# Attention and a two-layer GEMM in one kernel: earlier w_in, later w_out, another order of the second GEMM's filling

## The chip, the cores and the metric

One NeuronCore of a Trainium2 chip runs the whole kernel. The metric is the device time of one execution in microseconds; a lower one is better.

## The reference

```python
# q, k, v: (8, 8, 576, 64) fp32; f: (8, 8, 576)
scores = matmul(q, k.T) / sqrt(64)
cum = cumsum(log(clip(f, 1e-4, 1)), axis=-1)
decay = cum[:, :, :, None] - cum[:, :, None, :]
attn = softmax(where(causal, -1e9, scores + decay))
x = matmul(attn, v)            # -> (4608, 512): heads side by side
h = x @ w_in                   # w_in (512, 2048)
out = gelu(h) @ w_out          # w_out (2048, 512), exact gelu; out fp32
```

## The kernel before

The decay splits into a factor for the row, which the normalisation takes out again, and one for the column, which is multiplied into v. So GpSimd or VectorE *weighs* v (`weigh_v`, L228: two heads at a time, bf16, with the weights themselves as a 65th column), and the attention is exp of the scaled scores, a triangular mask, a matmul with the weighed v and a division by the 65th column.

The kernel works on eight batches of 576 tokens for the attention and on nine chunks of 512 tokens for the GEMMs. One batch has four pairs of heads `i`. For a pair there are four score tiles `t` (`scores`, L246): matmuls of kT and qA/qB into a PSUM tile with tag "s" (two buffers), ScalarE's exponential to a tile `e{t}`, GpSimd's mask of the diagonal blocks (L263, one or two instructions). `attend` (L275) multiplies these with the weighed v into a tile with tag "o" (two buffers), `normalize` (L290) divides on VectorE, and `to_xT` (L303) transposes x on TensorE and copies it to `xT_sb`.

`gemm1(c, ffb)` (L314) is one of 16 blocks of the first GEMM: four matmuls of 512 columns into a PSUM tile with tag "m" (two buffers), then gelu on ScalarE into `g_of[c][ffb]`. `gemm2(c)` (L332) is a generator over the 64 matmuls of the second GEMM, four tiles of 128 tokens one after the other with 16 matmuls each; a copy on VectorE and a store on SyncE's queue follow each tile. `take(gen, n)` issues the next n of them.

The order within each engine is the order of the program text. Batch 0 has its own text, `first_attention` (L359). Then, for b = 1 to 7, `attention(b, gemm2(b-1), counts)` (L422) runs with the second GEMM of the chunk before as filling: after score tile t of pair i stand `counts[i][t]` of its matmuls (lists FILL for b = 2 to 7 and FILL_1 for b = 1, L419; row 4 of a list is the end of the attention; what is left over comes at the very end). After each attention comes `gemm1(b, ...)`; among its blocks stand the transposes of q and k of the next batch (`transposes_pe`, L193: TensorE into a buffer with tag "s", eight copies on VectorE) and the weighings of the next batch (blocks 2, 6, 10, 14, on GpSimd). In the first GEMM of chunk 0 the transposes of pairs 0, 1 and 2 of batch 1 stand at blocks 8, 11 and 15; those of pair 3 stand within the attention of batch 1 and use the tag "o".

Which of two buffers a PSUM tile gets is fixed when the program is built, and the waits for it with it.

There are two DMA queues. SyncE's (hardware) loads f and v and stores the result. v has one buffer in `v_pool`, so v of batch b+1 starts when the last weighing of batch b has read its own. GpSimd's (software) loads q, k, w_in and w_out and casts them to bf16; an issue takes GpSimd's time and stands in its order. In `first_attention`, w_in (`load_w_in`, four issues) stands behind `weigh_v(0, 1)`, so behind the first half of v of batch 0. `load_next` issues q and k of batch 1 in two halves of the heads and then w_out (`load_w_out`, four issues of four row blocks); v of batch 1 follows on SyncE's queue in five issues (`load_v(1)`, L455).

Of the kernel before, what the change touches and what calls it, by code (L numbers as in the profile page):

```python
# [8 lines left out]
FP32 = mybir.dt.float32  # L9
# [5 lines left out]
P = 128  # L15
# [34 lines left out]
def kernel(  # L50
# [10 lines left out]
    nc = tc.nc  # L61
# [3 lines left out]
    d_model, d_ff = moe_w_in.shape  # L65
    N_tok = B * S
    n_dm = d_model // P
    n_ff = d_ff // P
    n_sub = TC // P
# [19 lines left out]
    def load_qk_tokens(b, h0=0, h1=H):  # L89

        if b not in qk_of:
            qk_of[b] = [
                qk_pool.tile([PT, H, JT * D], BF16, tag=n, name=f"{n}{b}")
                for n in "qk"
            ]
        for src, dst in zip((q, k), qk_of[b]):
            nc.gpsimd.dma_start(  # L97
                dst[:, h0:h1, :],
                src[b, h0:h1].rearrange("h (p j) d -> p h (j d)", j=JT),
            )  # L100

    def load_v(b, h0=0, h1=H):
        if b >= B:
            return
        if b not in v_of:
            v_of[b] = v_pool.tile([P, H, NBLK, D], FP32, tag="v", name=f"v{b}")
        for n in range(NBLK):
            nc.sync.dma_start(  # L108
                v_of[b][:, h0:h1, n, :],
                v[b, h0:h1, K0[n] : K0[n] + P].rearrange("h p d -> p h d"),  # L110
            )
# [26 lines left out]
    w_out_sb = consts.tile([P, n_ff, d_model], BF16)  # L138
# [3 lines left out]
    def load_w_in(c):  # L142
        f4 = slice(c * d_ff // 4, (c + 1) * d_ff // 4)
        nc.gpsimd.dma_start(w_in_sb[:, :, f4], w_in_r[:, :, f4])

    def load_w_out():
        for kt in range(0, n_ff, 4):
            nc.gpsimd.dma_start(w_out_sb[:, kt : kt + 4, :], w_out_r[:, kt : kt + 4, :])
# [79 lines left out]
    def weigh_v(b, i, eng=None):  # L228

        if b not in vw_of:  # L230
            vw_of[b] = v_pool.tile([P, H, NBLK, D + 1], BF16, tag="vw", name=f"vw{b}")
        hs = slice(2 * i, 2 * i + 2)
        bh = b * H + 2 * i
        w = wT[:, :, bh : bh + 2].rearrange("p n h -> p h n")
        eng = eng or nc.gpsimd
        eng.tensor_tensor(  # L236
            vw_of[b][:, hs, :, 0:D],
            v_of[b][:, hs, :, :],
            w.unsqueeze(3).to_broadcast([P, 2, NBLK, D]),
            Alu.mult,  # L240
        )
        eng.tensor_copy(vw_of[b][:, hs, :, D], w)
# [3 lines left out]
    def scores(b, i, t):  # L246
        st = s_psum.tile([P, 2, 512], FP32, tag="s", name=f"s{t}")
        c = 0
        for n, q0, w in STILES[t]:
            for h, qt in enumerate((qA[i], qB[i])):  # L250
                nc.tensor.matmul(  # L251
                    st[:, h, c : c + w],
                    kT[i][:, K0[n] : K0[n] + P],
                    qt[:, q0 : q0 + w],
                    start=True,
                    stop=True,
                )
            c += w
        et = e_pool.tile([P, 2, 512], BF16, tag=f"e{t}", name=f"e{t}")
        e_of[b, i, t] = et  # L260
        nc.scalar.activation(et[:, :, 0:c], st[:, :, 0:c], Act.Exp, scale=scale)  # L261
        for c0 in SDIAG[t]:
            nc.gpsimd.affine_select(  # L263
                out=et[:, :, c0 : c0 + P],
                in_=et[:, :, c0 : c0 + P],
                compare_op=Alu.is_ge,
                fill=0.0,
                base=0,
                pattern=[[0, 2], [1, P]],
                channel_multiplier=-1,  # L270
            )
# [57 lines left out]
            ]  # L329
        nc.scalar.activation(g_of[c][ffb], ps, Act.Gelu)  # L330

    def gemm2(c):  # L332

        t0 = c * TC
        for ts in range(n_sub):
            ps = m_psum.tile([P, d_model], FP32, tag="m", name="ps2")
            for kt in range(n_ff):
                nc.tensor.matmul(  # L338
                    ps,
                    g_of[c][kt][:, ts * P : (ts + 1) * P],  # L340
                    w_out_sb[:, kt, :],
                    start=(kt == 0),
                    stop=(kt == n_ff - 1),
                )
                if kt == n_ff - 1:
                    ot = o_pool.tile([P, d_model], FP32, tag="ot", name="ot")
                    nc.vector.tensor_copy(ot, ps)  # L347
                    nc.sync.dma_start(
                        out[t0 + ts * P : t0 + (ts + 1) * P, :], ot
                    )  # L350
                yield

    def take(gen, n):
        for _ in range(n):
# [2 lines left out]


    def first_attention():  # L359
        def load_next():  # L360
            load_qk_tokens(1, 0, 4)
            load_qk_tokens(1, 4, 8)
            load_w_out()

        def transposes(i, pool, tag):
            transposes_first(i, 1, pool, tag)
            transposes_first(i, 0, pool, tag)

        def attend_pair(i):
            for h in range(2):  # L370
                attend(0, i, h, (0, 1, 2, 3, 4))
                normalize(0, i, h)

        transposes(0, o_psum, "o")
        scores(0, 0, 0)
        scores(0, 0, 1)
        transposes(1, m_psum, "m")
        psw = o_psum.tile([P, NBLK, BH], FP32, tag="o", name="psw")
        for n in range(NBLK):
            nc.tensor.transpose(  # L380
                psw[:, n, :], wk[:, K0[n] : K0[n] + P], ident_fp[:BH, :BH]
            )
        nc.vector.tensor_copy(wT[:, 0:4, :], psw[:, 0:4, :])
        nc.vector.tensor_copy(wT[D:P, 4, :], psw[D:P, 4, :])
        scores(0, 0, 2)
        scores(0, 0, 3)
        scores(0, 1, 0)
        scores(0, 1, 1)
        transposes(2, m_psum, "m")
        weigh_v(0, 0, nc.vector)  # L390
        weigh_v(0, 1)
        for c in range(4):
            load_w_in(c)
        scores(0, 1, 2)
        scores(0, 1, 3)
        scores(0, 2, 0)
        scores(0, 2, 1)
        transposes(3, m_psum, "m")
        attend_pair(0)
        weigh_v(0, 2, nc.vector)  # L400
        scores(0, 2, 2)
        scores(0, 2, 3)
        weigh_v(0, 3)
        to_xT(0, 0, m_psum, "m")
        scores(0, 3, 0)
        scores(0, 3, 1)
        attend_pair(1)
        scores(0, 3, 2)
        scores(0, 3, 3)
        load_next()  # L410
        attend_pair(2)
        to_xT(0, 1, m_psum, "m")
        attend_pair(3)
        to_xT(0, 2, m_psum, "m")
        to_xT(0, 3, m_psum, "m")

    FILL = [[0, 12, 4, 4], [2, 3, 3, 2], [2, 3, 3, 2], [2, 2, 2, 2], [8, 4, 4, 0]]  # L419
    FILL_1 = [[0, 4, 0, 0], [0, 4, 0, 4], [2, 2, 2, 2], [3, 3, 3, 3], [8, 4, 4, 0]]  # L420

    def attention(b, fill, counts):  # L422
        for i in range(HP):
            for t in range(4):
                scores(b, i, t)
                if i >= 2 and t == 0:
                    to_xT(b, i - 2)
                if i and t == 1:
                    attend(b, i - 1, 0, (0, 1, 2))
                elif i and t == 2:  # L430
                    attend(b, i - 1, 0, (3, 4))
                    normalize(b, i - 1, 0)
                elif i and t == 3:
                    attend(b, i - 1, 1, (0, 1, 2, 3, 4))
                    normalize(b, i - 1, 1)
                if b == 1 and i == 0 and t == 2:
                    transposes_pe(1, 3, in_s=False)
                    load_qk_tokens(2)
                take(fill, counts[i][t])
        i = HP - 1  # L440
        take(fill, counts[HP][0])
        attend(b, i, 0, (0, 1, 2, 3, 4))
        normalize(b, i, 0)
        to_xT(b, i - 1)
        take(fill, counts[HP][1])
        attend(b, i, 1, (0, 1, 2, 3, 4))
        normalize(b, i, 1)
        take(fill, counts[HP][2])
        to_xT(b, i)
        take(fill, 999)  # L450

    for b in range(B):
        if b == 0:
            first_attention()
            load_v(1)  # L455
        else:
            load_v(b + 1)
            attention(b, gemm2(b - 1), FILL_1 if b == 1 else FILL)
        for ffb in range(n_ff):
            gemm1(b, ffb)  # L460
            if b + 1 < B:
                at = (8, 11, 15) if b == 0 else (0, 4, 8, 11)
                if ffb in at:
                    transposes_pe(b + 1, at.index(ffb))
                if ffb % 4 == 2:
                    weigh_v(b + 1, ffb // 4)
        if 0 < b < B - 2:
            load_qk_tokens(b + 2)
    take(gemm2(B - 1), 999)
# [34 lines left out]
```

## Time and profile before

| | us |
|---|---|
| median of 3 runs | 399.92 (399.39 to 400.99) |
| the profiled execution | 400.63 |
| its span, first to last instruction | 398.8 |
| TensorE busy | 369.6 (93%) |
| ScalarE busy | 217.8 (55%) |
| VectorE busy | 203.3 (51%) |
| GpSimd busy | 130.2 (33%) |

The first row stands for the kernel, the second and third for the one execution that the trace shows. Busy times are of an engine over the whole span. The ends of matmuls are modelled and overlap the next one's start, so TensorE's busy time is not its time at full rate.

### The profile page before, as it was taken

To read this page: it belongs to the slowest core of one execution; us is meant where nothing else is said; L and a number is where in the kernel's file an instruction comes from. 1 tells how busy PE (TensorE), PEld (TensorE's weight loads), DVE (VectorE), ACT (ScalarE), POOL (GpSimd) and SP (SyncE) were. 2 spreads that over 40 slices of the span, in tenths; PEclk is the share of its full clock that TensorE was granted. 3 is DMA by queue.
4 is the path that set the end of the run, shared out by engine and by line. 5 is a ranking of instruction groups with operands and counts; after the bars stand their busy time and mean duration, and the time that the engine had idled before them with its cause. 6 is when DMAs were issued, how large, how long until landed. Compare 5 with 4: busy or idle time off the path is not lost.

```text
span 398.8 us, 7577 instructions
## 1 busy us (share of the span) xinstructions
PE 369.6 (93%) x3093; PEld 207.7 (52%) x3093; DVE 203.3 (51%) x448; ACT 217.8 (55%) x293; POOL 130.2 (33%) x261
## 2 busy tenths in 40 slices
PE   2889967999899999999999989999999999999995
PEld 1564434655466546654565546554665466444442
DVE  6473862449535863488247924693459535002011
ACT  4665561706764576646672677357745674630710
POOL 6586037350343323251335133612352142000000
PEclk9999966999999999999999999999999999999999
DMA  7899958727810781148402870178010010001002
GB/s 109 158 173 211 196 96 141 139 81 131 118 54 28 147 123 42 48 100 128 78 28 74 135 125 28 54 131 138 36 54 2 1 54 28 26 27 65 16 28 79
DMA packets 63874, 34.18 MB, mean 86 GB/s; under 512 B 42784, under 2 KB 59168, under 8 KB 63840
## 3 DMA queue, kind: packets, MB, share of 16 engines
q0 software_dynamic: 16896, 13.63, 22.9%
q1 hardware_dynamic: 46944, 20.08, 20.6%
q8 instruction: 24, 0.39, 0.4%
q14 instruction: 10, 0.08, 0.1%
HBM read 37.90 MB, written 9.44 MB: 119 GB/s over the span
## 4 chain that ended last, share of the span: by engine, by line
PE 79%; DVE 8%; DMA 6%; POOL 2%; issue 2%; SPq 1%; ACT 1%; POOLq 0%
PE ps L338 31%; PE ps L318 23%; PE s L251 11%; PE o L282 7%; DMA v<-in_v_dram 5%; PE s_t L209 3%; DVE kT L221 3%; PE ps_x L306 2%; SPq L108 1%; POOL vw L236 1%; DVE qA L221 1%; DVE ot L347 1%; PE ps_f L174 1%; ACT e L261 1%; DVE qB L221 1%
## 5 line engine op out<-in xcount | busy, mean ns | idle before, releaser
L338 PE MATMUL ps<-w_out_sb,g 128*128 128x512 bf16 x576 | 145.4, 383 | 0.0
L330 ACT ACTIVATE g<-ps 128x512 bf16<-128x512 f32 x144 | 86.0, 598 | 106.1 <-PE ps L318 106.1
L261 ACT ACTIVATE e<-s 128x1024 bf16<-128x1024 f32 (+2 forms) x128 | 107.3, 863 | 52.5 <-PE s L251 47.9
L318 PE MATMUL ps<-xT_sb,w_in_sb 128*128 128x512 bf16 x576 | 131.1, 379 | 0.6
L263 POOL TENSOR_SCALAR_AFFINE_SELECT e<-e 128x256 bf16<-128x256 bf16 x160 | 63.7, 413 | 115.0 <-ACT e L261 113.8
L318 PEld LDWEIGHTS <-w_in_sb 128*128 128x128 bf16 x576 | 54.5, 98 | 60.7 <-issue 0.6
L338 PEld LDWEIGHTS <-g 128*128 128x128 bf16 x576 | 50.7, 98 | 42.9 <-issue 1.8
L251 PE MATMUL s<-qA,kT 128*128 128x384 bf16 (+2 forms) x192 | 56.0, 299 | 12.3 <-DVE kT L221 6.9
L347 DVE COPY ot<-ps 128x512 f32<-128x512 f32 x36 | 24.8, 690 | 82.1 <-PE ps L338 81.1
L251 PEld LDWEIGHTS <-kT 128*128 128x128 bf16 x384 | 37.8, 103 | 47.6 <-DVE kT L221 8.0
L221 DVE COPY kT<-s_t 64x288 bf16<-64x288 bf16 x108 | 51.8, 479 | 1.5
L236 POOL TENSOR_TENSOR vw<-v,wT 128x640 bf16<-128x640 f32 x30 | 38.3, 1277 | 42.5 <-PE o L282 22.6
L251 PE MATMUL s<-qB,kT 128*128 128x384 bf16 (+2 forms) x192 | 51.6, 300 | 0.3 <-DVE qB L182 0.3
L282 PE MATMUL o<-vw,e 128*128 128x65 bf16 x960 | 45.2, 196 | 4.5 <-POOL e L263 4.3
L282 PEld LDWEIGHTS <-e 128*128 128x128 bf16 x960 | 41.6, 99 | 12.7 <-POOL e L263 5.4
L295 DVE RECIPROCAL r<-o 128x5 f32<-128x5 f32 x64 | 12.5, 195 | 69.4 <-PE o L282 69.3
L221 DVE COPY qA<-s_t 64x288 bf16<-64x288 bf16 x54 | 25.8, 479 | 14.5 <-PE s_t L209 13.5
L296 DVE TENSOR_TENSOR x<-o,r 128x320 bf16<-128x320 f32 x64 | 31.5, 492 | 2.2
L221 DVE COPY qB<-s_t 64x288 bf16<-64x288 bf16 x54 | 26.0, 481 | 0.7
L97 POOL DMA_DIRECT2D q<-in_q_dram x12 | 9.1, 757 | 45.7 <-PE s_t L209 44.7
L309 DVE COPY xT_sb<-ps_x 128x576 bf16<-128x576 bf16 x32 | 14.5, 452 | 8.3 <-PE ps_x L306 8.3
L306 PE MATMUL ps_x<-ident_bf,x 128*128 128x128 bf16 x160 | 14.4, 220 | 1.8 <-DVE x L296 1.8
(49 smaller groups left out, 133.8 us busy)
## 6 DMA issues: line engine op xcount, KB each, us to landing
out_dram<-ot SPq DMA_DIRECT2D x36, 256.0 KB, 2.0
v<-in_v_dram SPq DMA_DIRECT2D x35, 256.0 KB, 4.8
q<-in_q_dram POOLq DMA_DIRECT2D x6, 576.0 KB, 6.4
k<-in_k_dram POOLq DMA_DIRECT2D x6, 576.0 KB, 8.4
w_in_sb<-in_moe_w_in_dram POOLq DMA_DIRECT2D x4, 512.0 KB, 8.0
w_out_sb<-in_moe_w_out_dram POOLq DMA_DIRECT2D x4, 512.0 KB, 17.3
v<-in_v_dram SPq DMA_DIRECT2D x10, 128.0 KB, 5.4
q<-in_q_dram POOLq DMA_DIRECT2D x4, 144.0 KB, 4.0
```

Of the source, the lines that this page charges most:

```text
L221: nc.vector.tensor_copy(rows[:, odd], ps[odd * D : (odd + 1) * D, h].rearrange("d j p -> d p j"),)
L236: eng.tensor_tensor(vw_of[b][:, hs, :, 0:D], v_of[b][:, hs, :, :], w.unsqueeze(3).to_broadcast([P, 2, NBLK, D]), Alu.mult,)
L251: nc.tensor.matmul(st[:, h, c : c + w], kT[i][:, K0[n] : K0[n] + P], qt[:, q0 : q0 + w], start=True, stop=True,)
L261: nc.scalar.activation(et[:, :, 0:c], st[:, :, 0:c], Act.Exp, scale=scale)
L263: nc.gpsimd.affine_select(out=et[:, :, c0 : c0 + P], in_=et[:, :, c0 : c0 + P], compare_op=Alu.is_ge, fill=0.0, base=0, pattern=[[0, 2], [ ...
L282: nc.tensor.matmul(o[:, m, :], e_of[b, i, t][:, h, c : c + P], vw_of[b][:, 2 * i + h, n, :], start=(n == 0), stop=(n == m),)
L296: nc.vector.tensor_tensor(x_of[b, i][:, :, h, :], o[:, :, 0:D], r.unsqueeze(2).to_broadcast([P, NBLK, D]), Alu.mult,)
L306: nc.tensor.transpose(ps[:, K0[m] : K0[m] + P], x_of[b, i][:, m, :, :], ident_bf)
L318: nc.tensor.matmul(ps, w_in_sb[:, kt, ffb * P : (ffb + 1) * P], xT_sb[:, kt, t0 : t0 + TC], start=(kt == 0), stop=(kt == n_dm - 1),)
L330: nc.scalar.activation(g_of[c][ffb], ps, Act.Gelu)
L338: nc.tensor.matmul(ps, g_of[c][kt][:, ts * P : (ts + 1) * P], w_out_sb[:, kt, :], start=(kt == 0), stop=(kt == n_ff - 1),)
L347: nc.vector.tensor_copy(ot, ps)
```

## The change

- `load_w_in` moves up in `first_attention`: from behind `weigh_v(0, 1)` to behind `scores(0, 0, 2)`, so it no longer stands behind a weighing that waits for v.
- `load_w_out` moves from behind q and k of batch 1 to block 2 of the first GEMM of chunk 0, behind `weigh_v(1, 0)` in GpSimd's order.
- v of batch 1 is loaded in two halves of the heads, five issues each.
- The transposes of q and k of batch 1 stand at blocks 10, 13 and 15 instead of 8, 11 and 15.
- `gemm2` of chunk 0 runs in quarters of w_out: two tiles of tokens are open at once, and each quarter of four row blocks is used for both before the next quarter. The other chunks keep their order.
- FILL's first row is 5, 7, 4, 4 instead of 0, 12, 4, 4. FILL_1 has nothing in its first pair and 2, 2, 2, 2 in the three others.

```diff
-    def gemm2(c):
+    def gemm2(c, quarters=False):
+        if quarters:
+            order = [
+                (t2 + ts, 4 * kq + kt)
+                for t2 in (0, 2)
+                for kq in range(4)
+                for ts in range(2)
+                for kt in range(4)
+            ]
+        else:
+            order = [(ts, kt) for ts in range(n_sub) for kt in range(n_ff)]
...
-            load_w_out()
...
         scores(0, 0, 2)
+        for c in range(4):
+            load_w_in(c)
         scores(0, 0, 3)
...
         weigh_v(0, 1)
-        for c in range(4):
-            load_w_in(c)
...
-        load_next()
+        load_qk_tokens(1, 0, 4)
+        load_qk_tokens(1, 4, 8)
...
-    FILL = [[0, 12, 4, 4], [2, 3, 3, 2], [2, 3, 3, 2], [2, 2, 2, 2], [8, 4, 4, 0]]
-    FILL_1 = [[0, 4, 0, 0], [0, 4, 0, 4], [2, 2, 2, 2], [3, 3, 3, 3], [8, 4, 4, 0]]
+    FILL = [[5, 7, 4, 4], [2, 3, 3, 2], [2, 3, 3, 2], [2, 2, 2, 2], [8, 4, 4, 0]]
+    FILL_1 = [[0, 0, 0, 0], [2, 2, 2, 2], [2, 2, 2, 2], [2, 2, 2, 2], [8, 4, 4, 0]]
...
-            load_v(1)
+            load_v(1, 0, 4)
+            load_v(1, 4, 8)
...
-            attention(b, gemm2(b - 1), FILL_1 if b == 1 else FILL)
+            attention(b, gemm2(b - 1, b == 1), FILL_1 if b == 1 else FILL)
...
-                at = (8, 11, 15) if b == 0 else (0, 4, 8, 11)
+                at = (10, 13, 15) if b == 0 else (0, 4, 8, 11)
...
                     weigh_v(b + 1, ffb // 4)
+                if b == 0 and ffb == 2:
+                    load_w_out()
```

## Rows read from the trace of the kernel before

**Rows 1.** The page's 40 slices of the span: TensorE's granted clock, in tenths.

```profile
PEclk9999966999999999999999999999999999999999
```

**Rows 2.** TensorE's waits, 33 to 103 us: total us, times, longest us.

```profile
PE o L282 <- POOL e L263: 4.3, 2, 3.9
```

**Rows 3.** TensorE's waits, 98 us to the end.

```profile
PE s L251 <- DVE kT L221: 6.0, 6, 1.0
```

**Rows 4.** GpSimd in order of time: start, us, work, count [idle before, releaser].

```profile
14.57 0.79 POOL L263 TENSOR_SCALAR_AFFINE_SELECT e<-e 128x256 bf16<-128x256 bf16 x2 [2.50 <-ACT e L261]
...
19.24 3.06 POOL L144 DMA_DIRECT2D w_in_sb<-in_moe_w_in_dram  x4
...
33.36 3.02 POOL L148 DMA_DIRECT2D w_out_sb<-in_moe_w_out_dram  x4
56.36 1.28 POOL L236 TENSOR_TENSOR vw<-v,wT 128x640 bf16<-128x640 f32 x1 [19.98 <-DMA v<-in_v_dram]
...
61.87 1.49 POOL L263 TENSOR_SCALAR_AFFINE_SELECT e<-e 128x256 bf16<-128x256 bf16 x4
```

**Rows 5.** SyncE's queue in order of time: issues of v, batch 1.

```profile
28.46 10.53 SPq L108 DMA_DIRECT2D v<-in_v_dram  x5
```

**Rows 6.** DMA: packets by queue, 40 to 50 us; the page's median landing.

```profile
q1 hardware_dynamic: 1606, 0.40, 30.7%
q0 software_dynamic: 1605, 1.53, 91.2%
...
w_in_sb<-in_moe_w_in_dram POOLq DMA_DIRECT2D x4, 512.0 KB, 8.0
w_out_sb<-in_moe_w_out_dram POOLq DMA_DIRECT2D x4, 512.0 KB, 17.3
```

**Rows 7.** TensorE in order of time, batch 0 to the first GEMM of chunk 1.

```profile
26.98 1.11 PE L282 MATMUL o<-vw,e 128*128 128x65 bf16 x30
...
49.42 0.34 PE L251 MATMUL s<-qA,kT 128*128 128x384 bf16 x1 [0.91 <-DVE kT L221]
...
52.50 0.53 PE L251 MATMUL s<-qA,kT 128*128 128x448 bf16 x1 [2.47 <-ACT e L261]
...
54.91 0.47 PE L251 MATMUL s<-qA,kT 128*128 128x320 bf16 x1
...
57.14 0.48 PE L251 MATMUL s<-qA,kT 128*128 128x384 bf16 x1
...
62.34 0.29 PE L282 MATMUL o<-vw,e 128*128 128x65 bf16 x2 [3.91 <-POOL e L263]
...
68.71 0.33 PE L251 MATMUL s<-qA,kT 128*128 128x384 bf16 x1
...
73.08 0.33 PE L251 MATMUL s<-qA,kT 128*128 128x384 bf16 x1
...
86.97 1.03 PE L318 MATMUL ps<-xT_sb,w_in_sb 128*128 128x512 bf16 x4
```

**Rows 8.** VectorE in order of time: copies of the transposes for batch 1.

```profile
41.47 0.97 DVE L221 COPY qA<-s_t 64x288 bf16<-64x288 bf16 x2 [7.89 <-PE s_t L209]
...
51.36 1.95 DVE L221 COPY kT<-s_t 64x288 bf16<-64x288 bf16 x4
```

**Rows 9.** TensorE by stretch: length, busy (count), granted clock, DMA share, GB/s.

```profile
57.00:58.00 1.00, 1.00 (x7) 0.60 0.00 0
```

**Rows 10.** TensorE in order of time, start of the attention of batch 2.

```profile
103.22 0.22 PE L251 MATMUL s<-qB,kT 128*128 128x128 bf16 x1
104.44 0.36 PE L251 MATMUL s<-qA,kT 128*128 128x448 bf16 x1 [1.00 <-DVE kT L221]
...
104.83 2.75 PE L338 MATMUL ps<-w_out_sb,g 128*128 128x512 bf16 x12
107.42 0.30 PE L251 MATMUL s<-qA,kT 128*128 128x320 bf16 x1
```

**Rows 11.** ScalarE in order of time: the first exponential of batch 2.

```profile
104.95 1.02 ACT L261 ACTIVATE e<-s 128x1024 bf16<-128x1024 f32 x1
```

More of the change, by code (lines that the diff above doesn't have):

```diff
@@ L330, in gemm1 @@
         nc.scalar.activation(g_of[c][ffb], ps, Act.Gelu)
-    def gemm2(c):
+    def gemm2(c, quarters=False):
         t0 = c * TC
[L335 to L351, printed above, removed]
+        if quarters:
[8 more added lines that the diff above has]
+            order = [(ts, kt) for ts in range(n_sub) for kt in range(n_ff)]
+        pss = {}
+        for ts, kt in order:
+            if kt == 0:
+                pss[ts] = m_psum.tile([P, d_model], FP32, tag="m", name="ps2")
+            nc.tensor.matmul(
+                pss[ts],
+                g_of[c][kt][:, ts * P : (ts + 1) * P],
+                w_out_sb[:, kt, :],
+                start=(kt == 0),
+                stop=(kt == n_ff - 1),
+            )
+            if kt == n_ff - 1:
+                ot = o_pool.tile([P, d_model], FP32, tag="ot", name="ot")
+                nc.vector.tensor_copy(ot, pss[ts])
+                nc.sync.dma_start(out[t0 + ts * P : t0 + (ts + 1) * P, :], ot)
+            yield
     def take(gen, n):
@@ L359, in first_attention @@
     def first_attention():
-        def load_next():
-            load_qk_tokens(1, 0, 4)
-            load_qk_tokens(1, 4, 8)
-            load_w_out()
         def transposes(i, pool, tag):
```

## The prediction

> **What bounds the kernel now.** I read the views from coarse to fine. First the granted clock in the 40 slices of the span: it stands at its high level everywhere but in two slices, 50 to 70 us [rows 1]. So there is one disturbed place, and behind it a regular part. Then TensorE's waits of the two parts. From 33 to 103 us, TensorE stood 4.3 us for GpSimd's masks, 3.9 of it in one piece [rows 2]. From 98 us on it waited six times in all, 1.0 us each, always the same way: a score tile for VectorE's copies [rows 3]. Apart from these it is busy, so TensorE sets the end: whatever closes a wait of TensorE, or gives it back its clock, comes off the time one for one; what only moves work of other engines does not.
>
> Next, where the big wait comes from. GpSimd's order of time shows it: the weighing of v for batch 1 stood 19.98 us for the transfer of v, until 56.36 us, four weighings then ran (1.38 us each), and only behind them, at 61.87 us, came the masks of batch 1's first score tiles [rows 4]. So `attend` could start only at 62.34 us, after 3.91 us idle [rows 7]. The transfer is slow because it shares: from 40 to 50 us the software queue (w_out) moved 1605 packets and the hardware queue (v) 1606. One packet goes against one, and the packets are of 953 and 250 bytes (1.53 MB and 0.40 MB by those counts) [rows 6]. v gets 160 packets per us, and the five issues that make up v of batch 1, from 28.46 us on [rows 5], are 1.31 MB, 5120 packets of 256 bytes.
>
> **The change, part by part.**
>
> *w_in earlier.* Its four issues took 3.06 us of GpSimd from 19.24 us on, behind the weighing of heads 2 and 3. Now they stand behind the mask of the third score tile, the first of the two at 14.57 us [rows 4]. So they run from 15.0 to 18.0 us; the fourth tile's mask, three others (0.4 us each) and that weighing (1.4 us) follow, and it ends near 21.0 us instead of 19.24. Its first reader is `attend_pair(1)` at 26.98 us [rows 7], so 6 us cover it, and I cost it at nothing; only a delay beyond that would show, one for one. The gain is on the DMA side: the software queue gets w_in 4.2 us earlier; its last part, issued at 17.2 us, lands some 8.0 us later (median) [rows 6], so before 28 us.
>
> *v before w_out.* w_out's four issues stood at 33.36 us, right behind those of q and k [rows 4]; now they stand behind the first weighing of batch 1, which waits for heads 0 to 3 of v. In GpSimd's queue only the three other weighings and then the masks of batch 1 are behind it. When do the 2560 packets of that half land? The trace shows no v of batch 1 without traffic beside it, so I bound it: it costs nothing before GpSimd is there (33.4 us), and at 160 packets per us from its issue at 28.5 us it is over by 44.5. I take 35, near the early end, because w_in is then over and q and k, the only others, are issued just before 33.4. So w_out is issued at 36.5 to 39.5, at the late end 46 to 49. At the same 8.0 us the first quarter of w_out is there between 45 and 57 us. Its first use, below, is at 58.2. I cost it at nothing. The second half of v, another 2560 packets, runs against q, k and w_out, and at 160 per us lands near 51 us. Two weighings (3 us) and four masks of 0.37 us [rows 4] follow, done by 55.5; `attend` comes at about 59.7, so the cover is 4 us. The 3.91 us wait is gone.
>
> *Transposes of batch 1 at blocks 10, 13, 15 instead of 8, 11, 15.* This costs something. One block of the first GEMM is 4 x 0.216 = 0.86 us (twelve such matmuls from 104.83 to 107.42) [rows 10]. VectorE's copies began at 41.47 us, and the three sets follow each other without a break until 51.36 + 1.95 = 53.31 us [rows 8], 3.95 us a set. Two blocks later they begin at 43.2, and the sets end at 47.1, 51.1 and 55.05. The first score tile of batch 1 waited for the second set's end and started at 49.42; now it starts at 51.16, 1.74 us later. The second tile came 3.08 us after the first (a table load and an exponential between them) [rows 7], so now at 54.24. The third tile then needs the third set and comes at 55.1; without the four matmuls of gemm2 that stood there, the way from it to the next pair of heads is that of before, 57.14 - 54.91 = 2.23 us [rows 7], and 0.15 more because the exponential of the third tile queues behind that of the second. The next pair begins at **57.5 us, against 57.14**. The moved transposes and the dropped matmuls cancel up to then.
>
> *The rest of chunk 1.* From 57.5 us nothing should wait any more. The pace is in the trace: pair 2 took 73.08 - 68.71 = 4.37 us with 8 matmuls of gemm2, the counts that pair 1 now has, and in it a transpose of x that pair 1 doesn't have, five times 128 columns, 0.27 us at 0.216 for 512: 4.1 us. From 68.71 to the next first GEMM at 86.97 are 18.26 us, with 52 of the 64 matmuls [rows 7]. Now 56 fall there: 18.26 + 4 x 0.216 = 19.1. Together 23.2 us. To this comes the clock. In the trace it was at its low level while TensorE worked without a break from 52.50 on, and came back at 57.8: the mean from 57 to 58 us is 0.60, between 0.5 and 1 [rows 9]. That is 5.3 us of matmuls. Now the matmuls run without a real gap from 54.24, so the clock should return between 57.8 and 60 us, and not fall again. Between 57.5 and 59.2 matmuls take twice as long: 0.85 us lost, bounds 0.15 and 1.3. So gemm1 of chunk 1 starts at 57.5 + 23.2 + 0.85 = 81.5 us instead of 86.97: **5.4 us gained**, bounds 4.5 and 6.5 with half a microsecond for the timing of pair 0.
>
> *Weight quarters.* They are the same 64 matmuls and 64 weight loads in another order, with two accumulators open instead of one. The third tile of tokens needs the first one's buffer; by columns from a copy of 288 (0.49 us) [rows 8] a copy out takes at most 0.87 us, and four matmuls of the second tile (0.86 us) run beside it. Nothing, and where it is longer some tenths, once. As w_out has landed by 57 us at the latest, the quarters hide nothing either: they are an insurance.
>
> *Counts 5 and 7 instead of 0 and 12, chunks 2 to 7.* The last matmul of the first tile is issued at 103.22 and takes its 0.06 us; the second tile starts at 104.44, the row says 1.00 us idle [rows 10]. As the ends of matmuls overlap in this profile, the time without an issue is 104.44 - 103.28 = 1.16 us. Five matmuls of gemm2 fill 5 x 0.216 = 1.08 of it. Their inputs are the gelu outputs of blocks 0 to 4, long done, and an accumulator that block 14 left. Then the second tile goes at 104.44 as before, followed by 7 matmuls and not 12, and the third tile at 106.34, not 107.42. It needs the first tile's buffer, free at 104.95 + 1.02 = 105.97 [rows 11]; the cover is 0.37 us. The fourth tile comes at 107.6, when two exponentials (at most 2 x 1.02 from 104.95) are over by 107.0. So 1.08 us stay, in each of the six chunks that show this wait [rows 3]: **6.5 us gained**; by the row's own idle time it would be 6.0, and 7.0 if the whole 1.16 counted.
>
> **Sum.** 5.4 + 6.5 = 11.9 us. The profiled execution took 400.63 us with a span of 398.8, so 388.7 with a span near 386.9. That execution lies 0.71 above the median of 399.92, so a median of **388.0**. Own range: gains of 4.5 + 6.0 to 6.5 + 7.0, that is 386.4 to 389.4.
>
> **Rivals.**
> - *v's second half lands late, and GpSimd's queue is still the wait.* For it: one packet against one, and w_out is on its way from 40 us. If v shared from its first packet, 5120 packets at 160 per us would end at 60.5 us, the masks at 65, 5.4 us after `attend` wants them. Below a landing at 55 us it costs nothing. Against it: w_in is over by 28. 389.5 to 393.5.
> - *The fill at the first tile brings nothing or costs.* The buffer that the second tile takes is fixed when the program is built. In batch 1 it waited 2.47 us for ScalarE, that is for the first tile's own exponential [rows 7], and not for VectorE. If five matmuls between the tiles make chunks 2 to 7 like that, the second tile waits until 106.03 and the third comes at 106.03 + 0.39 + 1.51 = 107.9, 0.5 us later than now: six times 0.5 lost instead of six times 1.08 gained, 397.6; with gain and loss even, 394.5. Against it: there the copies ended after the exponential, here 1.6 us before it.
> - *Slower: w_out turns into the wait.* If the first half of v came as late as the whole does now (56.36), w_out would be issued from 57.7 on, land between the 8.0 us of w_in and the 17.3 of w_out [rows 6] later, near 70, and TensorE, whose queue is in order, would stand before its first gemm2 matmul from 58.2 on. Then come the 23.2 us less 0.7, and 2.5 for the clock: gemm1 of chunk 1 at 95, 8 us later than now. That eats the 6.5 of the fill and 1.5 more: 401.4; at w_out's 17.3 us it is 406. Below a landing at 55 us it is no slower than before. Against it: w_in is done before v starts. 403.5 as a middle.
> - *The clock swings in the quarter order*, because the two accumulators alternate every four matmuls. At the low level the 64 matmuls take another 13.8 us: 401.8. The first GEMM alternates two accumulators every four matmuls too, and the clock is at its high level there (slices 4, 5, 9 and 10, counted from one) [rows 1]. The Trainium skill speaks for this rival (TensorE: Matmul & The Clock Gate, section A second HAM failure mode: psum-queue depth-cycling): at 512 columns, cycling through accumulator banks makes TensorE idle briefly between groups, often enough that the clock swings between its levels. The trace of this kernel disagrees, so I give it little.
>
> **How the numbers follow.** Forecast 0.77; late v 0.09; fill without gain 0.06; w_out as the wait 0.05, most of it slower; clock 0.03. A measurement of this kernel tells about 0.5% from no change, 2 us: faster below 397.9, slower above 401.9. Faster is then 0.77 + 0.09 + 0.06 = 0.92; the same 0.04 and slower 0.04 share the last two. The range takes the forecast's own and most of the late v, with half a microsecond below for a clock that never falls: 385.8 to 392.0, about 0.85.
>
> **What will show it.** Right: TensorE's wait for VectorE in chunks 2 to 7 gone from the waits, and each of these chunks 1.08 us shorter; no wait of `attend` for GpSimd; gemm1 of chunk 1 at 81 to 82.5 us; the first score tile of batch 1 near 51.2. Wrong: a wait of TensorE on w_out, GpSimd waiting for v past 55 us, the second tile of a chunk released by ScalarE, or the low clock beyond 60 us.

## The result, and the profile after

The changed kernel takes 389.02 us (median of four runs, 388.05 to 389.12) against 400.11 us for the kernel before, run beside it: a ratio of 0.9717, with a 95% interval of 0.9691 to 0.9742. The forecast was 388.0, with a range of 385.8 to 392.0. The profiled execution took 389.12 us with a span of 387.2, 11.6 less than before. The times of kernels here and below are medians of their undisturbed runs.

The 40 slices come first, as in [rows 1] (a slice is now 9.7 us). Where two slices stood at 6 tenths, two now stand at 7 and 8:

```profile
PEclk9999978999999999999999999999999999999999
```

The largest of TensorE's waits over the whole span are these (total us, times, longest us; two lines of 0.3 and 0.2 us are left out). [rows 2] and [rows 3] had a wait of `attend` (L282) for GpSimd's masks and six waits for VectorE's copies. Both are gone. What is left behind the first 33 us is one wait for VectorE of 2.6 us and one for ScalarE of 2.5 us, where the kernel before had 0.91 and 2.47 [rows 7]:

```profile
PE ps_f L174 <- DMA k<-in_k_dram: 5.6, 1, 5.6
PE s L251 <- ACT e L261: 4.3, 4, 2.5
PE s L251 <- DVE kT L221: 2.6, 1, 2.6
PE ps_x L306 <- DVE x L296: 2.1, 2, 1.4
PE s L251 <- DVE kT L182: 1.3, 1, 1.3
```

TensorE in order of time shows where these two are (start, us, work, count, idle before). It answers [rows 7]; the last five lines answer [rows 10]:

```profile
51.12 0.34 PE L251 MATMUL s<-qA,kT 128*128 128x384 bf16 x1 [2.64 <-DVE kT L221]
...
54.20 0.53 PE L251 MATMUL s<-qA,kT 128*128 128x448 bf16 x1 [2.47 <-ACT e L261]
...
57.25 0.48 PE L251 MATMUL s<-qA,kT 128*128 128x384 bf16 x1
...
62.85 0.33 PE L251 MATMUL s<-qA,kT 128*128 128x384 bf16 x1
...
82.18 1.02 PE L318 MATMUL ps<-xT_sb,w_in_sb 128*128 128x512 bf16 x4
...
98.04 0.33 PE L251 MATMUL s<-qA,kT 128*128 128x384 bf16 x1
...
98.48 1.24 PE L350 MATMUL ps<-w_out_sb,g 128*128 128x512 bf16 x5
99.64 0.36 PE L251 MATMUL s<-qA,kT 128*128 128x448 bf16 x1
...
101.54 0.30 PE L251 MATMUL s<-qA,kT 128*128 128x320 bf16 x1
...
139.02 0.33 PE L251 MATMUL s<-qA,kT 128*128 128x384 bf16 x1
```

The same stretch of the kernel before began with this line, ahead of those in [rows 10]:

```profile
102.84 0.33 PE L251 MATMUL s<-qA,kT 128*128 128x384 bf16 x1
```

The first GEMM of chunk 1 starts at 82.18 instead of 86.97 us: the start gave 4.79 us. In chunk 2 the second score tile still comes 1.60 us after the first (99.64 - 98.04; before 104.44 - 102.84), but five matmuls now lie in between, and the third comes 3.50 us after the first instead of 4.58. The gain is 1.08 us a chunk; from one first tile to the next it is 139.02 - 98.04 = 40.98 us, against 144.89 - 102.84 = 42.05 before. Six times 1.08 and 4.79 are 11.3 of the 11.6 us of the span; the rest lies behind the last matmul.

GpSimd in order of time answers [rows 4]. The weighing of v for batch 1 now waits 3.71 us and 0.97 us instead of 19.98, all four are done by 46.8 us, and the masks of batch 1 wait for nothing but the exponentials, from 54.22 us on:

```profile
14.90 3.02 POOL L144 DMA_DIRECT2D w_in_sb<-in_moe_w_in_dram  x4
...
37.05 1.28 POOL L236 TENSOR_TENSOR vw<-v,wT 128x640 bf16<-128x640 f32 x1 [3.71 <-DMA v<-in_v_dram]
...
38.42 3.05 POOL L148 DMA_DIRECT2D w_out_sb<-in_moe_w_out_dram  x4
...
43.91 1.28 POOL L236 TENSOR_TENSOR vw<-v,wT 128x640 bf16<-128x640 f32 x1 [0.97 <-DMA v<-in_v_dram]
...
54.22 0.77 POOL L263 TENSOR_SCALAR_AFFINE_SELECT e<-e 128x256 bf16<-128x256 bf16 x2 [7.48 <-ACT e L261]
```

### The profile page after: what moved, and what is told of

It reads as the page before. It is cut to its first block, busy times and chain, and to the rows that moved or that the text cites. A ratio compares the mean times of both kernels' runs of the same rounds, so it can differ in the third digit from the quotient of the medians.

```text
span 387.2 us, 7532 instructions
## 1 busy us (share of the span) xinstructions
PE 363.6 (94%) x3040; PEld 205.7 (53%) x3093; DVE 204.0 (53%) x448; ACT 217.8 (56%) x293; POOL 130.9 (34%) x261
## 4 chain that ended last, share of the span: by engine, by line
PE 90%; DVE 5%; ACT 2%; issue 1%; DMA 1%; ACTq 0%
PE ps L350 32%; PE ps L318 31%; PE s L251 13%; PE o L282 7%; PE s_t L209 3%; PE ps_x L306 2%; DVE ot L359 1%; ACT e L261 1%; PE ps_f L174 1%; DVE x L296 1%; DVE xT_sb L309 1%; DMA f_sb<-in_f_dram 1%; DVE kT L221 0%; DVE cum L161 0%; ACT L261 0%
## 5 line engine op out<-in xcount | busy, mean ns | idle before, releaser
L350 PE MATMUL ps<-w_out_sb,g 128*128 128x512 bf16 x540 | 138.9, 380 | 1.7
L221 DVE COPY kT<-s_t 64x288 bf16<-64x288 bf16 x108 | 51.8, 480 | 1.5
L236 POOL TENSOR_TENSOR vw<-v,wT 128x640 bf16<-128x640 f32 x30 | 38.4, 1280 | 27.0 <-PE o L282 22.3
L282 PEld LDWEIGHTS <-e 128*128 128x128 bf16 x960 | 40.6, 98 | 8.1 <-DVE x L296 1.3
L282 PE MATMUL o<-vw,e 128*128 128x65 bf16 x960 | 43.9, 194 | 0.1
L306 PE MATMUL ps_x<-ident_bf,x 128*128 128x128 bf16 x160 | 14.4, 220 | 2.1 <-DVE x L296 2.1
```

The lines of the kernel that those rows point to most:

```text
L221: nc.vector.tensor_copy(rows[:, odd], ps[odd * D : (odd + 1) * D, h].rearrange("d j p -> d p j"),)
L236: eng.tensor_tensor(vw_of[b][:, hs, :, 0:D], v_of[b][:, hs, :, :], w.unsqueeze(3).to_broadcast([P, 2, NBLK, D]), Alu.mult,)
L282: nc.tensor.matmul(o[:, m, :], e_of[b, i, t][:, h, c : c + P], vw_of[b][:, 2 * i + h, n, :], start=(n == 0), stop=(n == m),)
L306: nc.tensor.transpose(ps[:, K0[m] : K0[m] + P], x_of[b, i][:, m, :, :], ident_bf)
L350: nc.tensor.matmul(pss[ts], g_of[c][kt][:, ts * P : (ts + 1) * P], w_out_sb[:, kt, :], start=(kt == 0), stop=(kt == n_ff - 1),)
```

## The experiments

Three questions: do the two gains stand alone and add up; which of the moved transfers brings the gain of the start; and what do the two waits that are left cost, with the low clock behind them. The kernel before took 400.1 to 400.6 beside them. Runs of one kernel spread by about 1 us (388.05 to 389.12 for the changed one), so a difference of some tenths between two kernels tells nothing.

### The two gains alone

The kernel before with the new first row of FILL:

```diff
-    FILL = [[0, 12, 4, 4], ...
+    FILL = [[5, 7, 4, 4], ...
```

> The kernel before with only FILL's first row changed to 5, 7, 4, 4. My theory: TensorE's wait of 1.0 us before the second score tile goes in each of the six chunks, 1.08 us a chunk, 6.5 in all, so about 393.6 against 400.1; the start of the kernel stays as it was, with the first GEMM of chunk 1 at 87. Rival: the fill only moves the wait to the next tile, 399 to 400.

Measured: 393.97 us, ratio 0.9838 (0.9824 to 0.9853). The first GEMM of chunk 1 starts at 87.16 us (86.97 before).

The changed kernel with the old first row (the same lines the other way round):

> The changed kernel with FILL's first row back at 0, 12, 4, 4. My theory: the parts add up, so the six waits of 1.0 us come back and it takes 6.5 more than the changed kernel, about 395.5; the first GEMM of chunk 1 stays at 82.2. Rival: the two gains share something, and it is nearer to 390 or 398.

Measured: 394.65 us, ratio 0.9855 (0.9838 to 0.9871). The waits from 98 us to the end are back as they were in [rows 3]:

```profile
PE s L251 <- DVE kT L221: 5.9, 6, 1.0
```

That is 5.6 us more than the changed kernel, not 6.5. The missing 0.9 is not in the fill. From the first score tile of chunk 2 to the last second GEMM this kernel takes 375.10 - 97.21 = 277.89 us and the changed one 369.50 - 98.04 = 271.46, a difference of 6.43. In this run the start was 0.84 us shorter (first GEMM of chunk 1 at 81.34); the section on the prediction shows where.

The changed kernel with two matmuls in the wait instead of five:

```diff
-    FILL = [[5, 7, 4, 4], ...
+    FILL = [[2, 10, 4, 4], ...
```

> The changed kernel with FILL's first row 2, 10, 4, 4: two matmuls in the wait instead of five. My theory: each matmul in the wait gives back its 0.216 us, so three fewer cost 3 x 0.216 x 6 = 3.9 us, about 392.9, and a wait of some 0.6 us stays in each chunk. Rival: any work between the tiles is enough, and it stays at 389.

Measured: 392.48 us. The same stretch takes 372.57 - 97.23 = 275.34 us, 3.88 more than in the changed kernel, and six waits of 0.6 us stay:

```profile
PE s L251 <- DVE kT L221: 3.4, 6, 0.6
```

So each matmul that is put into the wait gives back its own 0.216 us, and the two gains add up.

### Which transfer it was

w_out back behind q and k of batch 1, the rest as changed:

```diff
         load_qk_tokens(1, 4, 8)
+        load_w_out()
...
-                if b == 0 and ffb == 2:
-                    load_w_out()
```

> The changed kernel with w_out issued behind q and k of batch 1 as before, so without the gate on v. My theory: w_out flows only behind q and k on its queue, near 40 us with or without the gate; w_in early and v in halves already make v early enough, and the time stays at 389.0 within 0.5. Rival: the gate is what brings v forward; without it the masks of batch 1 are late again, attend waits, and it takes 392 to 393.

Measured: 388.93 us, no different from 389.02. GpSimd shows that the gate (w_out's place behind a weighing that waits for v) does something all the same: without it the second half of v lands near 53 us. In the changed kernel it lands near 44, and between 46 and 52 in four kernels below that have the same loads.

```profile
53.43 1.28 POOL L236 TENSOR_TENSOR vw<-v,wT 128x640 bf16<-128x640 f32 x1 [12.85 <-DMA v<-in_v_dram]
```

But the weighings end at 56.2 us, and `attend` has not come yet.

w_in back behind the weighing of heads 2 and 3, the rest as changed:

```diff
         scores(0, 0, 2)
-        for c in range(4):
-            load_w_in(c)
...
         weigh_v(0, 1)
+        for c in range(4):
+            load_w_in(c)
```

> The changed kernel with w_in issued behind the weighing of heads 2 and 3 as before. My theory: w_in ends near 32 us instead of 28, the first half of v lands near 38 and the second near 51, GpSimd is done with the weighings at 54 and attend comes at 59.7: no TensorE wait, 389.0 within 0.5. Rival: the second half lands behind 55 us, attend waits for the masks, 390 to 393.

Measured: 388.28 us. Again nothing is lost: the first weighing of batch 1 starts at 41.20 us instead of 37.05, and the last is over by 49.9, still ahead of `attend`.

Both back (the two edits together), v in halves as changed:

> The changed kernel with w_in and w_out both at their old places; v of batch 1 stays in two halves. My theory: each of the two moves alone leaves the other as cover, and without both v shares with the software queue from its first packet to its last, as before. The first half lands near 38 us and its two weighings go early, the second lands near 55 to 56, two weighings and three masks are over at about 60.6, and attend, due at 59.7, waits about 1 us: 389.5 to 391. Rival: the loads were never the point, since GpSimd's wait was covered by other changes; 388.5.

Measured: 391.31 us, ratio 0.9770 (0.9741 to 0.9799), so 2.3 us over the changed kernel and a little more than I expected. GpSimd shows why:

```profile
56.96 1.28 POOL L236 TENSOR_TENSOR vw<-v,wT 128x640 bf16<-128x640 f32 x1 [13.26 <-DMA v<-in_v_dram]
...
59.71 1.49 POOL L263 TENSOR_SCALAR_AFFINE_SELECT e<-e 128x256 bf16<-128x256 bf16 x4
61.14 0.84 POOL L97 DMA_DIRECT2D q<-in_q_dram  x1
61.97 0.78 POOL L97 DMA_DIRECT2D k<-in_k_dram  x1
62.75 1.84 POOL L263 TENSOR_SCALAR_AFFINE_SELECT e<-e 128x256 bf16<-128x256 bf16 x5
```

The second half of v lands near 57 us, the first masks come at 59.71, as expected; but the issues of q and k of batch 2 stand between them and the mask of the fourth tile, which starts only at 62.75. TensorE's `attend` waits three times, 2.2 us in all (0.89, 0.48 and 0.81).

All loads as before: both back, and v of batch 1 in five whole issues.

```diff
-            load_v(1, 0, 4)
-            load_v(1, 4, 8)
+            load_v(1)
```

> The changed kernel with w_in, w_out and v of batch 1 all loaded as before (v in five whole issues); the fill counts, the transposes and the quarters stay. My theory: GpSimd waits for v until 56.3 us, four weighings run to 61.9 and the masks behind them to 63; attend, due at 59.7, waits 2.7 to 3.5 us, the low clock lasts longer, and the first GEMM of chunk 1 comes at 85 to 87 instead of 82: 391.5 to 393.5. Rival: the new order of the fill alone brings what the start gained, and it stays at 388 to 389.

Measured: 394.76 us, ratio 0.9855 (0.9828 to 0.9881). It is above my 391.5 to 393.5, and 0.8 us above the kernel before with the new fill alone (393.97): the start's gain is gone altogether. The first GEMM of chunk 1 comes at 87.42 us, behind this wait of `attend`:

```profile
62.85 0.29 PE L282 MATMUL o<-vw,e 128*128 128x65 bf16 x2 [4.78 <-POOL e L263]
...
87.42 1.02 PE L318 MATMUL ps<-xT_sb,w_in_sb 128*128 128x512 bf16 x4
```

It is 0.87 us longer than the 3.91 us of [rows 7]: TensorE stands ready 0.36 us earlier than there, and the first masks come 0.52 us later (62.39 against 61.87). Behind it the granted clock is low a second time, from 60.2 to 67.0 us.

So without the three edits of the loads nothing of the start's gain is left, but no single one of the two moves carries it: w_in early and w_out late are each enough while v comes in halves. Both away costs 2.3 us; with v whole it costs 5.7. What v whole would cost with both moves kept was not run, nor were FILL_1's old counts alone.

### The quarters

```diff
-            attention(b, gemm2(b - 1, b == 1), FILL_1 if b == 1 else FILL)
+            attention(b, gemm2(b - 1), FILL_1 if b == 1 else FILL)
```

> The changed kernel with gemm2 of chunk 0 in the plain order. My theory: w_out has landed by 55 us and is first used at 58, so the quarters hide nothing and the time stays at 389.0 within 0.5. Rival: the last quarter is late for the plain order (its matmuls 12 to 15 come at about 62 us), 390 or more. Second rival: alternating the accumulators costs clock, and the plain order is faster by some us.

Measured: 388.40 us. The plain order is as fast. In the changed kernel w_out's issues landed 7.9 to 14.4 us after 38.4 to 40.7 us, the last at 55, ahead of the first matmul of gemm2 at 58.05. The rival of the swinging clock is out as well: with the quarters it is low from 53.6 to 60.4 us, without them from 49.6 to 59.8, and in neither later.

### What was left at the start

The transposes of batch 1 where they were:

```diff
-                at = (10, 13, 15) if b == 0 else (0, 4, 8, 11)
+                at = (8, 11, 15) if b == 0 else (0, 4, 8, 11)
```

> The changed kernel with the transposes of batch 1 at blocks 8, 11, 15 as before. My theory: VectorE's copies are 1.74 us earlier, the first score tile of batch 1 starts at 49.4 instead of 51.1, and the first GEMM of chunk 1 comes 1.2 to 2.2 us earlier (the rest is where the clock comes back): 387 to 388. Rival: q and k of batch 1 have not landed at block 8 (40.8 us) and TensorE waits for them, 389 or more.

Measured: 385.84 us, ratio 0.9631 (0.9606 to 0.9657): 3.2 us faster than the changed kernel, more than I expected. The first score tile of batch 1 waits 0.92 us instead of 2.64, and the clock is low for a shorter time, from 53.1 to 56.5 us (TensorE by stretch: length, busy and count, granted clock, DMA share, GB/s; before them, TensorE in order of time):

```profile
48.75 0.34 PE L251 MATMUL s<-qA,kT 128*128 128x384 bf16 x1 [0.92 <-DVE kT L221]
...
78.89 1.02 PE L318 MATMUL ps<-xT_sb,w_in_sb 128*128 128x512 bf16 x4
```

```profile
53.00:54.00 1.00, 1.00 (x15) 0.56 1.19 255
...
56.00:57.00 1.00, 0.85 (x9) 0.73 1.22 244
```

In the trace the first GEMM of chunk 1 is 3.29 us earlier (78.89 against 82.18), and that has three parts. The issue of q of batch 1 already stood 0.64 us earlier, at 29.98 instead of 30.62 us: batch 0 ran that much faster in this run. The first score tile is 2.37 us earlier, so 1.73 of it is the edit, as forecast. The two first pairs took 5.74 + 5.08 us instead of 6.13 + 5.60, 0.91 less in spite of one more wait, of 0.32 us; the gain goes with the low clock, which in the changed kernel lasted from 53.6 to 60.4 us. TensorE waited on no transfer, so the rival of a late q or k is out, and the later place of the transposes bought nothing.

The transposes earlier still, and gemm2 matmuls in the first pair:

```diff
-    FILL_1 = [[0, 0, 0, 0], [2, 2, 2, 2], [2, 2, 2, 2], [2, 2, 2, 2], [8, 4, 4, 0]]
+    FILL_1 = [[10, 2, 4, 4], [2, 3, 3, 2], [2, 3, 3, 2], [2, 2, 2, 2], [4, 4, 4, 0]]
...
-                at = (10, 13, 15) if b == 0 else (0, 4, 8, 11)
+                at = (7, 10, 13) if b == 0 else (0, 4, 8, 11)
```

> The changed kernel with the transposes of batch 1 at blocks 7, 10, 13 and gemm2 matmuls in its first pair of heads (10, 2, 4, 4; then 10, 10, 8, 12, 4 at the end). My theory: the two waits of 2.5 us at the start of batch 1 and the low clock behind them are what is left of the start; VectorE's second set of copies ends at 48.5 us, so the first tile starts near 48.5, ten matmuls fill most of the wait for the first exponential, and the clock stays up: first GEMM of chunk 1 near 74.5 instead of 82.2, about 381.5. Rival: w_out's first quarters (landing from 46 us on) or q and k at block 7 (39.9 us) are late; then TensorE waits on a transfer and it gains less than 3 us or loses.

Measured: 382.34 us, ratio 0.9548 (0.9533 to 0.9562), 6.7 us faster than the changed kernel. It has two edits, the earlier transposes and the matmuls in the first pair, and no run parts them. The clock stays at its high level in all slices, and one wait is left at the start of batch 1:

```profile
PEclk9999999999999999999999999999999999999999
```

```profile
52.68 0.36 PE L251 MATMUL s<-qA,kT 128*128 128x448 bf16 x1 [1.19 <-DVE kT L221]
...
75.36 1.03 PE L318 MATMUL ps<-xT_sb,w_in_sb 128*128 128x512 bf16 x4
```

Five matmuls more in that wait:

```diff
-    FILL_1 = [[10, 2, 4, 4], [2, 3, 3, 2], ...
+    FILL_1 = [[15, 2, 2, 1], [2, 3, 3, 2], ...
```

> The kernel with matmuls in the first pair (382.3) with 15, 2, 2, 1 there instead of 10, 2, 4, 4. What waited there last was 1.2 us for VectorE's third set of copies at the second score tile. My theory: five matmuls more in that wait take 1.08 us of it, 381.2. Rival: the second quarter of w_out, which the matmuls 9 to 15 need at 51 us, lands later, and TensorE waits for it, 382 or more.

Measured: 381.24 us, ratio 0.9517 (0.9493 to 0.9542), the fastest of all, and 1.10 us below the one before, as forecast. Its trace isn't read here; the next kernel has the same first pair, and no wait of TensorE is in that pair.

That kernel, with three matmuls kept for the stretch behind the last transposes of x:

```diff
-    FILL = [[5, 7, 4, 4], [2, 3, 3, 2], [2, 3, 3, 2], [2, 2, 2, 2], [8, 4, 4, 0]]
+    FILL = [[5, 7, 4, 4], [2, 3, 3, 2], [2, 3, 3, 2], [2, 2, 2, 2], [8, 1, 4, 0]]
```

> The kernel with 15, 2, 2, 1 in the first pair (381.3) with FILL's last row 8, 1, 4, 0 instead of 8, 4, 4, 0, so that three matmuls of gemm2 stay for the stretch behind the last transposes of x. There the fourth matmul of the next first GEMM starts some 0.25 us late, for VectorE copies the last output tile before it copies x. My theory: the three matmuls cover that in the six chunks 2 to 7, 6 x 0.25 = 1.5 us, 379.8. In the first pair of batch 1 no wait of 1.2 us for VectorE is left. Rival: the normalisation, which the fewer matmuls between the last two heads cover less, becomes the wait, and it stays at 381.3 or is slower.

Measured: 383.28 us, 2.0 slower than the one before: a miss, and the rival's case. TensorE's waits from 85 us on, and TensorE in order of time at the end of batch 2's attention:

```profile
PE o L282 <- DVE x L296: 1.9, 6, 0.3
```

```profile
112.92 0.38 PE L350 MATMUL ps<-w_out_sb,g 128*128 128x512 bf16 x1
113.62 0.65 PE L282 MATMUL o<-vw,e 128*128 128x65 bf16 x15 [0.32 <-DVE x L296]
...
115.37 0.81 PE L350 MATMUL ps<-w_out_sb,g 128*128 128x512 bf16 x3
116.02 1.03 PE L318 MATMUL ps<-xT_sb,w_in_sb 128*128 128x512 bf16 x4
116.88 0.42 PE L209 MATMUL s_t<-ident_bf,q 96*128 96x96 bf16 x6
```

The stall that I meant to close is closed: the first GEMM's block runs its four matmuls in 0.86 us (116.88 - 116.02), where the changed kernel's takes 1.12 (124.01 - 122.89):

```profile
122.89 1.28 PE L318 MATMUL ps<-xT_sb,w_in_sb 128*128 128x512 bf16 x4
124.01 0.42 PE L209 MATMUL s_t<-ident_bf,q 96*128 96x96 bf16 x6
```

But the three matmuls had been covering a normalisation ahead of the last `attend`, and that wait now stands open in each of the six chunks. From the first tile of chunk 2 to the last second GEMM it takes 363.67 - 90.68 = 272.99 us, against 271.46 in the changed kernel: 0.25 us a chunk worse in the balance, 1.53 in all. The other 0.5 us of the 2.0 is not explained; in this run the clock was also low from 25.7 to 29.1 us, in batch 0, and the first score tile of batch 1 came at 49.17 us, against 48.72 in the kernel with ten matmuls.

## Why the prediction was right

*What bounds the kernel.* TensorE sets the end, and its waits come off one for one. This held for the fill: 3.88 us for eighteen matmuls of 0.216 us (3.89), 6.43 us for thirty (6.48). But I called TensorE busy apart from the waits for masks and for the copies of chunks 2 to 7, and left out there the two at the start of batch 1, of 0.91 and 2.47 us, which only my step on the transposes has. The change does not close them (2.64 and 2.47); the kernel that fills them and moves the transposes gained another 7.8 us (381.24).

*Fill.* The term was 6.5 us and measured 6.46 (380.76 - 102.84 = 277.92 us before, 369.50 - 98.04 = 271.46 after, from the first score tile of chunk 2 to the last second GEMM). The choice of 1.16 us without an issue over the 1.00 us of idle time that the row shows was right: five matmuls of 1.08 us fitted, and the second tile did not come later. The third tile's cover of 0.37 us held too. The rival of a wait for the first tile's exponential did not come about. The ends of the two stretches:

```profile
380.76 13.98 PE L338 MATMUL ps<-w_out_sb,g 128*128 128x512 bf16 x64
...
369.50 13.98 PE L350 MATMUL ps<-w_out_sb,g 128*128 128x512 bf16 x63
```

*Loads.* The wait of `attend` is gone, as forecast, and the covers that I named were there. Two readings were too simple. The first half of v landed near 37 us, not 35, and the second near 44, not 51 (46 to 52 in the other kernels with these loads). And I told the wait's end as the work of one sequence, w_in early and then v ahead of w_out, and w_in's move was argued on the DMA side alone; the runs show that each of the two moves is spare as long as the other is there and v is halved. I had costed w_in's issues, the gate and the quarters at nothing, and undoing each of them changed nothing that these runs can tell (388.3 to 388.9 against 389.0). One thing I did not see: the two low slices of [rows 1] are two low stretches, and the second, from 61.2 to 68.0 us, began within the wait of `attend`. It is gone with that wait (TensorE by stretch, kernel before):

```profile
61.00:62.00 1.00, 0.00 (x0) 0.61 0.00 0
...
68.00:69.00 1.00, 1.00 (x6) 0.98 1.27 194
```

*Transposes and the first pair.* The first score tile was forecast at 51.16 us and came at 51.12; the second 54.24 and 54.20; the next pair 57.5 and 57.25. The step held to a quarter of a microsecond. What I called cancelled was a real price: undoing the transposes' move alone gave 3.2 us. Of the 3.29 in the traces 1.73 is the time by which VectorE's copies are earlier, my figure; 0.91 lies in the two first pairs, with the shorter low clock, and 0.64 comes from batch 0, which has nothing to do with the edit.

*The clock: the term that was mis-sized.* I took 0.85 us for it, with bounds of 0.15 and 1.3. In the profiled run it came back at 60.4 and not 59.2 us, 6.2 us after the matmuls began at 54.20. A low clock beyond 60 us was one of my signs of being wrong; the time came out all the same, because the term is small:

```profile
53.00:54.00 1.00, 0.00 (x0) 0.79 1.25 269
...
60.00:61.00 1.00, 1.00 (x10) 0.80 0.98 116
```

From 57.25 to 60.4 at half speed is 1.6 us, 0.7 more than forecast, and that is all but 0.15 of what the step from 57.25 us to the first GEMM of chunk 1 took too long (24.93 us against 24.05). The start gave 4.79 us instead of 5.4. The step that did not hold is the one from 5.3 us of matmuls before the return in the kernel before to a return between 57.8 and 60 us here. The matmuls began again at 54.20 us in the changed kernel, 54.30 with the old fill and 54.66 with w_out back, and the clock came back 6.2, 4.3 and 3.2 us later. What sets the moment stays open; in these runs it came back earlier where it had fallen earlier, but in the plain order it fell at 49.6 and came back only at 59.8. So the size is not fixed either. The second pair of batch 1 has the same work in all these kernels; it took 5.60 us in the changed kernel, 4.67 with the old fill, 4.35 and 4.36 with w_out and w_in back. With the old fill the clock was low already from 51.7 us and high again at 58.6, in the last two low from 51.0 and high again at 57.9 and 57.8 (here the returns with the old fill and with w_out back):

```profile
58.00:59.00 1.00, 1.00 (x7) 0.72 0.99 225
...
57.00:58.00 1.00, 1.00 (x9) 0.57 0.57 132
```

An earlier fall costs time in the first pair instead, so the first GEMM of chunk 1 differs less: 82.18 in the changed kernel, 81.27 and 81.45 in these two, 81.34 with the old fill. That is the 0.84 us of the start that the sum of the two gains seemed to lack.

The sum was 11.9 us; 11.5 came between the profiled executions and 11.1 between the medians.

## What to carry to other kernels

A wait of the bounding engine can be filled from the work behind it, matmul by matmul, up to the time without an issue, which here was longer than the idle time of the row (1.16 against 1.00 us). Before moving that work, look which other wait it had been covering: three matmuls taken from one place closed a stall of 0.25 us and opened a larger one (113.62 - 113.14 = 0.48 us without an issue). And a cause that is undone alone and changes nothing may still be one of two that cover each other, so undo them together too.

## What the runs showed of the hardware

When the low clock comes back after a stretch of waits is not fixed by the program text. The changed kernel and the two with another first row of FILL have the same text up to batch 2, and their first score tile of batch 1 starts within 0.1 us (51.12 to 51.22); the clock fell at 53.6 us in the first and at 51.7 and 51.8 in the other two, and came back at 60.4, 58.6 and 58.6. Batch 0 has a scatter too: matmuls of 448 columns took 0.58 us at 20.4 us in the changed kernel, and 0.35 at 20.2 in the run with the transposes back, and behind this stretch that run is 0.64 us ahead. The granted clock reads 1.00 in these stretches of both, so near the start of the span the duration of a matmul of known width tells the level and that column does not. At the start of batch 1 the clock did not fall in the traces with ten or fifteen matmuls in the first pair, even though one wait of 1.19 us stayed in the first of these; both also have earlier transposes, so the matmuls alone are not shown to do it.
